# One kernel, attention and a gated feed-forward layer: the hand-written order of all engines reaches over three chunks of eight instead of two

## The chip, the cores and the metric

The kernel runs on one core of a Trainium2 chip. The metric is the device time of one execution in microseconds (us). A core has five engines with a queue each: TensorE (PE in the profile, its weight loads PEld), VectorE (DVE), ScalarE (ACT), GpSimd (POOL) and SyncE (SP, which here only issues DMAs). Each engine works through its own instructions in order; a semaphore makes one engine wait for another.

## What is computed

Local attention with block summaries, and behind it a feed-forward layer with a short convolution and a gate. 4 batches, 8 heads, 768 positions, 64 numbers a head; model width 512, inner width 1024.

```python
def _attn_ref(q, k, v):
    k_sum = k.reshape(B, H, nb, block, D).max(axis=3)       # block = 32
    v_sum = v.reshape(B, H, nb, block, D).mean(axis=3)
    scores_l = scale * np.matmul(q, k.transpose(0, 1, 3, 2))
    mask_l = np.abs(pos[:, None] - pos[None, :]) < window   # window = 16
    scores_s = scale * np.einsum('bhsd,bhnd->bhsn', q, k_sum)
    scores_s = scores_s + np.log(block)
    ...
    a = a / (np.sum(a, axis=-1, keepdims=True) + 1e-09)
    v_all = np.concatenate([v, v_sum], axis=2)
    return np.matmul(a, v_all)

def _moe_ref(x, w_in, conv_w, w_out):
    h = np.maximum(x @ w_in, 0.0)
    ...
    for k in range(K):                                       # K = 3
        conv_out += conv_w[k][None, None, :] * hp[:, k:k + S, :]
    gate = 1.0 / (1.0 + np.exp(-conv_out))
    return h * gate @ w_out
```

## The kernel before

**Tiling.** The work is cut into 8 chunks `c` of 384 positions, two for each batch. Attention of a chunk runs in four pairs of heads; pair `n` is numbered through all chunks, so pairs 0 to 3 belong to chunk 0, 4 to 7 to chunk 1, and so on (32 pairs). The feed-forward layer of a chunk runs in 8 units `u` of 128 inner columns. A product in float32 is made of three TensorE matmuls of rounded parts (high by high, high by low, low by high), so there are hi and lo copies of the weights, of the attention's result (`xh`, `xl`) and of the gated values.

**Steps.** The program is made of small steps, with a name and numbers each; one step is one call of a function:

- DMAs on SP's queue: `R` k, `T` v, `Q` q, `K` and `V` the windows of k and v, `M` the block means of v, `I` and `O` a piece of w_in or w_out, `C` the convolution's weights.
- weights, once: `z`, `lo`, `st` put a float64 word's two halves together (ScalarE, VectorE, VectorE), `hi` rounds (ScalarE), `wl` makes the low part (GpSimd). `wlo3` is w_out's fourth piece, `wli3` w_in's.
- attention of pair n: `ks` block maximum of k (VectorE), `win` and `kb` put window and block keys together, `vs` block sum of v (VectorE), `pv` its transposition (TensorE), `vm` the mean (ScalarE), `vb` (GpSimd). `qk` 24 score matmuls; six each of `mx` (mask and maximum, VectorE) and `ex` (exponential, ScalarE); `sm`, `rc`, `nr` normalise (ScalarE, VectorE, GpSimd or VectorE). `trJ` and `cpJ` with J = 2n, 2n+1 transpose a head and copy it out of PSUM (TensorE; ScalarE or VectorE); `av` 24 matmuls with v; `xh` and `xl` round the result (ScalarE, VectorE).
- feed-forward of chunk c, unit u: `f c.u.cc`, cc = 0 to 3, three matmuls each (L429); `re` the ReLU (ScalarE, L443); `ta` and two `cv` the three taps (ScalarE or VectorE L454, VectorE L463); `th` tanh (ScalarE, L474); `mu` the gate (VectorE, L481); `gh`, `gl` the two parts of the gated value (ScalarE L491, GpSimd L494).
- second product: `g st.u` three matmuls (L513) into output tile st of batch 0, `ob` its copy and store (ScalarE). A tile needs the units of the chunks that hold its 128 rows.
- `w n`: n matmuls on an idle tile into an unused PSUM tile.

A letter at the end of a name chooses the engine: a ScalarE, v VectorE, p GpSimd.

**Written order.** The string `ORDER` is a list of such steps. With `FIRST` = 2 the list holds the feed-forward steps of chunks 0 and 1, what they need, and attention as far ahead as a later unit expects it (qk up to pair 13, tr up to 24, av up to 11). `run` calls each step, and `tc.manual_schedule()` keeps the order of the list on every engine.

**Planner.** Chunks `FIRST` to 7 come from `unit`, eight units each. Unit u of chunk c has the number j = 8(c + 1) + 3 + u. `slot(j)` issues attention steps ahead: an even j the loads of pair j/2 + 2 and the scores of pair j/2, an odd j the loads and block sums of pair (j + 1)/2. `vs`, `pv`, `vm`, `ks` occur only for the first half of a batch (`at(n)[3] == 0`), that is pairs 16 to 19, 24 to 27 and so on. Then come four `f`, `re`, `ta`, `cv` and two to four steps of the second product. In these chunks only TensorE keeps the program's order; a planner, which works from its own costs, orders the other engines. In chunk `FIRST` the slot's steps carry an edge behind the last of the listed steps that return an instruction: the last DMA on SP, and the last `mu` on VectorE (`last`). In `unit`, for an odd j:

```python
            if c == FIRST:
                for x in last.values():
                    behind.enter_context(tc.issue_after(x))
            slot(j)
        ...
        elif c == FIRST and u == 0:
            slot_t(j)
```

So in chunk `FIRST`, unit 0, the order on TensorE is: what `slot(j)` puts there, then `slot_t(j)` (tr and cp of group j - 2), then the f steps.

**Buffers that matter.** PSUM: the f steps have three tiles (`f1`), scores two, the transposed weights (`pt`) one, `xp` and from pair 4 on `pv` one together (`x`), the second product one (`f2`). SBUF: tag `stage`, two buffers, holds w_out's pieces, v of odd batches' loads (`vt`) and one pair's keys in turn; `kw` three, `q` and `va` four, `kT` two, `t` three.

Of the kernel before, what the change touches and what calls it, by code (L numbers as in the profile page):

```python
# [58 lines left out]
ex4.1.2 mx5.0.0 cp6v nr3.1p vm3 av2 zo0 mx5.0.1 loo0 ex5.0.0 tr7 sto0 T8 xh2 f0.1.1 I5 cp7a
mx5.0.2 vb3 xl2 K7 hio0 mx5.1.0 wli4 ex5.0.2 w1 av3 Q7 mx5.1.1 vs9 ex5.0.1 ex5.1.0 f0.0.2  # L60
mx5.1.2 xh3 M4 loi7 f0.1.2 zi7 xl3 sm4 sti7 ex5.1.2 f0.0.3 O1 zi3 pv9 ed4 f0.1.3 loi3 re0.0 rc4
f0.2.0 sti3 R9 re0.1 ex5.1.1 nr4.0p ta0.0v f0.2.1 M5 ta0.1a cv0.0.0 kb6 hii3 tr8 nr4.1p f0.2.2
cv0.1.0 Q9 hii7 qk6 cv0.0.2 wli3 cp8a cv0.1.2 th0.0 f0.2.3 V4 sm5 mx6.0.0 th0.1 mu0.0 tr9 wli7
re0.2 mx6.0.1 f0.3.0 R8 mu0.1 zi5 mx6.0.2 M6 ta0.2a f0.3.1 loi5 Q8 mx6.1.0 cp9a rc5 f0.3.2 sti5
# [12 lines left out]
f1.2.0 zo4 mx9.1.0 f1.0.3 ex8.1.1 loo4 mx9.1.1 gh0.7 T10 f1.2.1 sto4 sm8 K11 re1.0 f1.1.3 rc8
gl0.7 vs11 ta1.0a f1.2.2 re1.1 g0.3 cv1.0.0 nr8.0p O5 hio4 mx9.1.2 M8 f1.2.3 gh0.6 cv1.0.2 kb10
V8 wlo4 ta1.1a pv11 ks11 tr16 ex9.0.2 qk10 th1.0 cv1.1.0 nr8.1p ex9.0.0 g0.4 mu1.0 ex9.1.1 gl0.6
cv1.1.2 cp16a f1.3.0 vm11 vs10 ex9.1.2 tr17 kb11 f1.3.1 th1.1 ex9.1.0 mx10.0.0 pv10 O7 mu1.1  # L80
f1.3.2 vm10 Q11 zo5 loo5 f1.4.0 V9 mx10.0.1 gh1.0 sto5 f1.3.3 M9 ex9.0.1 cp17v gl1.0 f1.4.1 K12
re1.2 mx10.0.2 V10 sm9 av8 ta1.2a rc9 mx10.1.0 Q12 nr9.0p ex10.0.2 mx10.1.1 cv1.2.0 Q14 f1.4.2
nr9.1p zo7 K13 cv1.2.2 tr18 f1.4.3 Q13 mx10.1.2 th1.2 loo7 qk11 hio5 mu1.2 xh8 cp18v wlo5 V11
f1.5.0 ex10.1.0 mx11.0.0 M10 tr19 xl8 ex10.0.1 f1.5.1 ex10.1.1 sto7 g0.5 hio6 K14 mx11.0.1 hio7
cp19v wlo6 f1.5.2 mx11.0.2 re1.3 av9 V12 mx11.1.0 ta1.3a mx11.1.1 wlo7 ex10.0.0 g0.6 cv1.3.0 V13
ex10.1.2 cv1.3.2 f1.5.3 M13 ex11.0.0 kb12 sm10 mx11.1.2 g0.7 gh1.2 rc10 M11 nr10.0p qk12 M12 ob0
gl1.2 th1.3 tr20 ex11.0.2 g1.0 mu1.3 K15 nr10.1p ex11.1.2 mx12.0.0 f1.6.0 cp20v ex11.1.1 kb13
gh1.3 g1.1 mx12.0.1 mx12.0.2 ex11.0.1 gl1.3 tr21 re1.4 f1.6.1 re1.5 ta1.4v g1.2 ex11.1.0 cv1.4.0
# [11 lines left out]
def attention_ffn(ctx, tc, qT, kT, vT, k_win, v_win, w_in, cwT, w_out, mask8, ident_in, out):  # L100
# [17 lines left out]
    idle = cp.tile([P, 512], mybir.dt.bfloat16, name="idle")  # L120
# [99 lines left out]
    def keys(n):  # L220
        if n not in kw:
            if n == NP - 1:
                t = sp.tile([P, 1024], F32, tag="stage", name=f"kw{n}", bufs=2)
# [49 lines left out]
        nc.vector.tensor_reduce(ks[b, p], kv, AX.X, ALU.max)  # L273

    def win(n):
        k = kt[n]
        k = bass.AP(tensor=k.tensor, offset=k.offset, ap=[list(k.ap[0]), [QB, CB], [1, WK]])
        (nc.gpsimd if n else nc.vector).tensor_copy(keys(n)[:, :, :WK], k)

    def kb(n):  # L280
        c, p, b, hf = at(n)
        nc.gpsimd.tensor_copy(
            keys(n)[:, :, WK:NK], ks[b, p].unsqueeze(1).to_broadcast([P, CB, NB])
        )

# [11 lines left out]
        nc.tensor.transpose(pvs[n][:NB, :P], vsum.pop(n), ident)

    def v_mean(n):
        c, p, b, hf = at(n)  # L300
        vm[b, p] = cp.tile([NB, P], F32, tag=f"vm{p}", name=f"vm{n}")
        nc.scalar.activation(vm[b, p], pvs.pop(n)[:NB, :P], AF.Copy, scale=1.0 / BLK)

    def vb(n):
        c, p, b, hf = at(n)
        nc.gpsimd.tensor_copy(
            va[n][WK:NK, :, :], vm[b, p].unsqueeze(1).to_broadcast([NB, CB, P])
        )

# [44 lines left out]
            accum_out=sm[n][:, h, i : i + 1],  # L354
        )

    def sums(n):
        nc.scalar.activation(sm[n], sm[n], AF.Copy, bias=1e-9)

    def rc(n):  # L360
        nc.vector.reciprocal(sm[n], sm[n])
# [50 lines left out]
    def xh(n):  # L412
        nc.scalar.copy(rows(n)[0], xp[n][:, :CH])

    def xl(n):
# [22 lines left out]
        hf = c % 2  # L438
        return CH - 1 + 2 * hf, (CH - 1) * hf

    def re(c, u):
# [1 line left out]
        nc.scalar.activation(h, h, AF.Relu)  # L443
# [46 lines left out]
    def gh(c, u):  # L490
        nc.scalar.copy(gate_rows("hi", c, u), conv[c, u])  # L491

    def gl(c, u):
        nc.gpsimd.tensor_tensor(  # L494
            gate_rows("lo", c, u),
            conv.pop((c, u)),
            gate_rows("hi", c, u).bitcast(F32),
            ALU.subtract,
        )
# [252 lines left out]
```

## Time and profile before

| what | value |
| --- | --- |
| time, median of 3 runs | 385.96 us (385.96, 385.96, 388.12) |
| the profiled execution | time 388.25 us, span 386.5 us, mean granted TensorE clock 0.987 |
| TensorE busy | 367.7 us (95%) in 3131 instructions |
| VectorE, ScalarE, GpSimd busy | 245.5 (64%), 250.4 (65%), 147.8 us (38%) |
| chain that ended last, largest shares | TensorE 74%, DMA 13%, VectorE 5%, ScalarE 5% |
| DMA | 56.35 MB, mean 146 GB/s over the span |

The span is the time from the first to the last instruction of the profiled execution; its time has 1.75 us around it. Busy shares are averages over very different stages, so the stretches of the span are read one by one. The page's second part shows this in 40 equal slices, each digit the busy share in tenths (PEclk is the granted TensorE clock, DMA the share of the 16 DMA engines):

```profile
PE   7787999989879999999989999999999999999996
DVE  4998999975875664786655555666656655465200
ACT  2996999978936877655577787666665743334211
PEclk9998999999969999999999999999999999999999
DMA  8999976898596445653332333242310000000011
```

Each digit stands for 9.7 us. Two slices have a lower clock, the fourth and the twelfth. In the first ten slices VectorE, ScalarE and DMA are about full; from the thirteenth on TensorE is.

### The profile page before, as it was taken

The page shows a single profiled execution, that of the slowest core. Times are in us where ns is not written, and L with a number is a line of the kernel's source. Part 1 is how long each engine was busy: PE and PEld are TensorE (multiplying, and loading weights), DVE is VectorE, ACT ScalarE, POOL GpSimd, SP SyncE. Part 2 cuts the span into 40 slices and gives each one's busy share as a digit, 9 for nine tenths or more (in the row PEclk, how much of TensorE's full clock was granted, in tenths as well). Part 3 has the DMA queues.
Part 4 walks back from the last instruction along what each step waited for, and adds up shares of the span by engine and source line. Part 5 has one row for each costly group of instructions (what it writes and reads, how often), then busy time and mean ns, then how long its engine had stood idle before and what let it go on. Part 6 is the DMA issues. An engine that isn't in the chain of part 4 may idle for free.

```text
span 386.5 us, 8769 instructions
## 1 busy us (share of the span) xinstructions
PE 367.7 (95%) x3131; PEld 314.4 (81%) x3135; DVE 245.5 (64%) x765; ACT 250.4 (65%) x796; POOL 147.8 (38%) x184
## 2 busy tenths in 40 slices
PE   7787999989879999999989999999999999999996
...
DVE  4998999975875664786655555666656655465200
ACT  2996999978936877655577787666665743334211
...
PEclk9998999999969999999999999999999999999999
DMA  8999976898596445653332333242310000000011
GB/s 290 380 323 366 278 256 217 263 309 241 155 307 189 130 140 152 189 162 111 98 122 92 119 97 125 68 124 76 105 65 2 30 24 5 27 30 27 27 56 54
DMA packets 27435, 56.35 MB, mean 146 GB/s; under 512 B 3136, under 2 KB 11520, under 8 KB 27392
## 3 DMA queue, kind: packets, MB, share of 16 engines
...
q14 instruction: 18, 0.15, 0.1%
...
## 4 chain that ended last, share of the span: by engine, by line
PE 74%; DMA 13%; DVE 5%; ACT 5%; issue 1%; POOL 0%; SPq 0%; ACTq 0%; DVEq 0%; POOLq 0%
PE f L513 31%; PE f L429 29%; DMA wo<-w_out 6%; PE xp L387 5%; PE pt L373 5%; PE pq L319 4%; DMA kw<-k_win 2%; DMA va<-v_win 2%; DVE t L463 2%; DMA raw_b<-vT 2%; ACT a L348 2%; ACT t L474 1%; DMA mask<-mask 1%; DVE t L481 1%; DVE ks L273 1%
## 5 line engine op out<-in xcount | busy, mean ns | idle before, releaser
L494 POOL TENSOR_TENSOR glo<-t,ghi 128x383 fp32r<-128x383 f32 (+1 forms) x64 | 65.0, 1016 | 121.2 <-ACT ghi L491 112.4
L429 PE MATMUL f<-xh,win_hi 128*128 128x384 f32 (+1 forms) x256 | 93.7, 366 | 0.6 <-DVE t L481 0.3
L429 PE MATMUL f<-xl,win_hi 128*128 128x384 f32 (+1 forms) x256 | 87.9, 343 | 0.0
L429 PE MATMUL f<-xh,win_lo 128*128 128x384 f32 (+1 forms) x256 | 87.6, 342 | 0.0
L463 DVE SCALAR_TENSOR_TENSOR t<-f,cw,t 128x382 f32<-128x382 f32 (+3 forms) x128 | 78.6, 616 | 13.5 <-ACT t L452 10.7
L348 ACT ACTIVATE a<-a,nm 128x120 f32<-128x120 f32 x192 | 73.7, 386 | 3.6 <-DVE nm L333 3.1
L513 PE MATMUL f<-wout_hi,ghi 128*128 128x512 f32 x192 | 75.9, 396 | 0.0
L513 PE MATMUL f<-wout_lo,ghi 128*128 128x512 f32 x192 | 75.4, 393 | 0.0
L513 PE MATMUL f<-wout_hi,glo 128*128 128x512 f32 x192 | 74.9, 391 | 0.0
L474 ACT ACTIVATE t<-t 128x383 f32<-128x383 f32 (+1 forms) x64 | 33.6, 525 | 44.8 <-DVE t L463 43.9
L365 POOL TENSOR_TENSOR a<-a,sm 128x360 f32<-128x360 f32 x61 | 48.5, 811 | 29.6 <-ACT f L443 16.5
L481 DVE SCALAR_TENSOR_TENSOR t<-t,f 128x383 f32<-128x383 f32 (+1 forms) x64 | 35.5, 554 | 31.0 <-ACT t L474 30.7
L429 PEld LDWEIGHTS f<-xh,win_hi 128*128 128x128 f32 x256 | 49.3, 192 | 5.6 <-DVE t L481 1.7
L429 PEld LDWEIGHTS f<-xl,win_hi 128*128 128x128 f32 x256 | 49.4, 193 | 1.3 <-DVE xl L417 0.2
L429 PEld LDWEIGHTS f<-xh,win_lo 128*128 128x128 f32 x256 | 49.2, 192 | 0.0
L333 DVE CUSTOM_DVE_ANT_0 a<-pq,mask 128x120 f32<-128x120 f32 x192 | 44.7, 276 | 0.7 <-PE pt L373 0.6
L513 PEld LDWEIGHTS f<-wout_hi,glo 128*128 128x128 f32 x192 | 36.2, 188 | 8.0
L443 ACT ACTIVATE f<-f 128x384 f32<-128x384 f32 (+1 forms) x64 | 30.3, 474 | 16.9 <-PE f L429 16.8
L513 PEld LDWEIGHTS f<-wout_hi,ghi 128*128 128x128 f32 x192 | 36.2, 189 | 5.9 <-ACT ob L523 0.3
L513 PEld LDWEIGHTS f<-wout_lo,ghi 128*128 128x128 f32 x192 | 36.3, 189 | 5.2
L373 PE MATMUL pt<-ident,a 128*120 128x128 f32 x192 | 33.2, 282 | 6.8 <-DVE aT L378 3.2
L491 ACT CAST ghi<-t 128x383 fp32r<-128x383 f32 (+1 forms) x64 | 32.6, 509 | 8.9 <-DVE t L481 8.6
...
## 6 DMA issues: line engine op xcount, KB each, us to landing
...
```

The costliest lines, as they stand in the source:

```text
L333: nc.vector.tensor_tensor_reduce(aa[n, h][:, i, :], pq[n][h][:, i * NK : (i + 1) * NK], mask[:, {(0, 0): 0, (1, 2): 2}.get((hf, i), 1), :] ...
L348: nc.scalar.activation(a, a, AF.Exp, bias=nm[n][:, h, i : i + 1], scale=-1.0, accum_out=sm[n][:, h, i : i + 1],)
L365: engine[e].tensor_tensor(a, a, sm[n][:, h, :].unsqueeze(2).to_broadcast([P, 3, NK]), ALU.mult)
L373: nc.tensor.transpose(pt[j][:NK, i * P : (i + 1) * P], a[:, i, :], ident)
L429: nc.tensor.matmul(f1ps[c, u][:, :n], w[:, u, cc, :], x[:, cc, :n], start=(cc == 0 and m == 0), stop=(cc == NCC - 1 and m == 2),)
L443: nc.scalar.activation(h, h, AF.Relu)
L463: nc.vector.scalar_tensor_tensor(t[:, i0:i1], f1ps[c, u][:, hf + k - 1 + i0 : hf + k - 1 + i1], cw[:, u, k : k + 1], t[:, i0:i1], ALU.mult ...
L474: nc.scalar.activation(t, t, AF.Tanh, scale=0.5)
L481: return nc.vector.scalar_tensor_tensor(t, t, 1.0, h, ALU.add, ALU.mult)
L491: nc.scalar.copy(gate_rows("hi", c, u), conv[c, u])
L494: nc.gpsimd.tensor_tensor(gate_rows("lo", c, u), conv.pop((c, u)), gate_rows("hi", c, u).bitcast(F32), ALU.subtract,)
L513: nc.tensor.matmul(f2ps[b, st], g[:, fc, ss], w[:, fc, :], start=(fc == 0 and m == 0), stop=(fc == NFC - 1 and m == 2),)
```

## The change

`FIRST` becomes 3 and the list is made anew, for chunks 0, 1 and 2. It has 1019 entries in place of 766 (counting the `w` entries, which stand for 38 and 35 idle matmuls). It is another order from its first steps on, not the old one with a tail. New in it are the steps of chunk 2, that is 32 f steps with all behind them, the second product's tiles 2 to 4 of batch 0 (`g2.*` to `g4.*`, `ob2` to `ob4`), the attention steps that the planner's slots 27 to 34 issued (qk 14 to 17, tr 25 to 32, av 12 to 15, the loads with them), and `ed12`. Chunks 3 to 7 come from `unit`, which is unchanged. The helper functions take an engine's letter in more places; the old engine is the default everywhere, and the new list has letters on `nr`, `cp` and `ta` alone, as the old list has. According to its description, chunk 3's first steps were weighed in the making of the new list.

```diff
-FIRST = 2
+FIRST = 3
...
-R0 Q0 R1 I0 I1 R2 Q1 ks0 R3 win0 Q2 kb0 qk0 T0 ks1 win1 C kb1 zi0 loi0 T1 mx0.0.0 ex0.0.0
...
+R0 R1 Q0 R2 I1 Q1 I0 win0 ks0 I2 Q2 ks1 T0 kb0 qk0 R3 kb1 ks2 win2 Q3 win1 mx0.0.0 ex0.0.0
...
+ta0.0v tr8 ex5.1.1 f0.2.3 cv0.0.0 ex5.1.2 ta0.1a loi7 cv0.0.2 kb6 hii3 nr4.1p w2 qk6 cv0.1.0 sm5
+th0.0 wli3 rc5 re0.2 cv0.1.2 zi7 mu0.0 cp8a sti7 w4 f0.3.0 ta0.2a wli4 mx6.0.0 th0.1 f0.3.1 vs11
+zo0 tr9 gh0.0 f0.3.2 mx6.0.1 O1 loo0 hii7 cv0.2.0 gl0.0 O2 f0.3.3 cp9a V4 mu0.1 ex6.0.1 nr5.0p
...
-f1.7.2 ta1.6a mx13.0.2 g1.5 ex12.1.2 cv1.6.0 xh10 tr23 cv1.6.2 gh1.5 g1.6 ex13.0.1 mx13.1.0
-gl1.5 xl10 f1.7.3 sm12 cp23a mx13.1.1 th1.6 g1.7 rc12 mx13.1.2 nr12.1p ex13.1.0 mu1.6 av11
-ex13.0.2 nr12.0p re1.7 gh1.6 ta1.7v tr24 ex13.1.2 gl1.6 cv1.7.0 ex13.1.1 ob1 cv1.7.2 th1.7 sm13
-xh11 rc13 mu1.7 nr13.1p xl11 gh1.7 nr13.0p cp24v gl1.7
...
+ob1 tr22 xl9 f1.7.2 mx13.0.0 gh1.4 cp22v g2.0 ta1.6a mx13.0.1 ex12.1.2 mx13.0.2 pv17 f1.7.3
+cv1.6.0 ex12.1.0 f2.0.0 vm17 sm12 gh1.5 rc12 av10 cv1.6.2 re1.7 gl1.5 vs16 tr23 M14 xh10 f2.0.1
...
+cv2.5.0 tr32 ex17.1.1 g4.6 cv2.5.2 ex17.0.0 ex17.1.2 cp32v f2.6.0 th2.4 g4.7 th2.5 mu2.4 xh15
+f2.6.1 mu2.5 xl15 f2.6.2 sm17 gh2.5 rc17 nr17.1p ob4 nr17.0p gh2.3 gh2.4 gl2.5 f2.6.3 re2.6
+gl2.4 ta2.6a gl2.3 cv2.6.0 cv2.6.2 f2.7.0 th2.6 f2.7.1 mu2.6 f2.7.2 f2.7.3 re2.7 gh2.6 ta2.7v
+gl2.6 cv2.7.0 cv2.7.2 th2.7 mu2.7 gh2.7 gl2.7
...
-    def hi(kind, fc):
-        nc.scalar.copy(parts(kind, fc)[0], wu[f"{kind}{fc}"].bitcast(F32))
+    def hi(kind, fc, e="a"):
+        copy[e](parts(kind, fc)[0], wu[f"{kind}{fc}"].bitcast(F32))
...
-    def re(c, u):
+    def re(c, u, e="a"):
         h = f1ps[c, u][:, : CH + 2 * (c % 2)]
-        nc.scalar.activation(h, h, AF.Relu)
+        if e == "a":
+            nc.scalar.activation(h, h, AF.Relu)
+        else:
+            nc.vector.tensor_scalar(h, h, 0.0, None, ALU.max)
```

The same form of edit is made in `wlo`, `win`, `kb`, `v_mean`, `vb`, `sums`, `xh`, `gh` and `gl`.

More of the change, by code (lines that the diff above doesn't have):

```diff
@@ L59 @@
[L59 to L64, printed above, removed]
@@ L77 @@
[L77 to L82, printed above, removed]
@@ L83 @@
[L83 to L88, printed above, removed]
@@ new lines @@
+mx9.0.0 ex8.1.1 ks10 gl0.4 pv8 f1.2.0 re1.0 sm8 g0.3 ta1.0a mx9.0.1 loo6 vm8 mx9.0.2 f1.2.1 zo6
+rc8 cv1.0.0 nr8.0p g0.4 re1.1 O7 mx9.1.0 cv1.0.2 ta1.1a kb10 M8 pv9 f1.2.2 nr8.1p mx9.1.1 gh0.7
+V8 cv1.1.0 tr16 th1.0 R11 gl0.7 f1.2.3 mx9.1.2 ex9.0.0 cv1.1.2 Q13 qk10 cp16a K11 mu1.0 th1.1
+sto6 f1.3.0 zo5 K13 mu1.1 tr17 re1.2 Q11 f1.3.1 hio6 loo5 M11 f1.4.0 sto5 zo7 T10 f1.3.2 vm9
+loo7 hio5 K12 f1.4.1 sto7 cp17a f1.3.3 ta1.2v wlo5 ex9.0.2 V11 ex9.1.0 av8 mx10.0.0 cv1.2.0
+ex9.0.1 V10 ex9.1.1 wlo6 ks11 g0.5 hio7 M9 f1.4.2 ex9.1.2 cv1.2.2 wlo7 g0.6 sm9 mx10.0.1 th1.2
@@ new lines @@
+Q12 mx10.0.2 gh1.1 f1.4.3 mu1.2 T17 ex10.0.1 rc9 g0.7 mx10.1.0 nr9.0p gh1.0 R17 mx10.1.1
+mx10.1.2 f1.5.0 kb11 ob0 gl1.1 vs10 V9 tr18 qk11 xh8 cp18v kb12 R16 ex10.0.2 g1.0 kb13 re1.3
+nr9.1p f1.5.1 ex10.1.1 K14 ta1.3a gl1.0 g1.1 gh1.2 cv1.3.0 f1.5.2 ex10.1.0 Q15 gl1.2 mx11.0.0
+cv1.3.2 g1.2 ex11.0.0 T16 ex10.1.2 mx11.0.1 tr19 mx11.0.2 th1.3 g1.3 mx11.1.0 re1.4 mu1.3
+ex10.0.0 f1.5.3 sm10 g1.4 ta1.4a rc10 mx11.1.1 nr10.0p cp19a mx11.1.2 f1.6.0 xl8 ex11.0.1
+cv1.4.0 qk12 re1.5 ex11.1.1 nr10.1v tr20 ta1.5a K15 pv10 f1.6.1 ex11.1.0 cv1.5.0 cp20a g1.5
@@ new lines @@
+xl10 ex13.0.1 kb15 gl1.4 tr24 g2.2 cp24v mx14.0.0 av11 mu1.6 mx14.0.1 tr25 cv1.7.0 xh11 V15 g2.3
+ex13.1.2 M12 xl11 f2.0.2 gh1.6 V13 cp25v ex13.1.0 g2.4 gl1.6 T18 mx14.0.2 ex13.0.0 mx14.1.0 K17
+cv1.7.2 f2.1.0 ex13.1.1 V14 mx14.1.1 sm13 f2.0.3 th1.7 Q17 rc13 nr13.0p ex14.0.1 pv16 mu1.7
+f2.1.1 ex14.0.0 mx14.1.2 g2.5 gh1.7 ex14.0.2 gl1.7 tr26 ex14.1.2 g2.6 re2.0 kb16 f2.2.0 ex14.1.0
+ta2.0v vm16 qk15 ex14.1.1 cv2.0.0 g2.7 mx15.0.0 nr13.1v f2.1.2 ob2 cv2.0.2 f2.2.1 ks17 f2.1.3
+cp26a th2.0 f2.2.2 mx15.0.1 kb17 mx15.0.2 re2.1 av12 sm14 ta2.1a tr27 V16 g3.0 mx15.1.0 M15
@@ new lines @@
+mx15.1.1 ex15.1.0 f2.2.3 mx15.1.2 Q18 cp27a mu2.0 g3.1 ex15.1.1 R18 rc14 nr14.0v re2.2 K18
+f2.3.0 xh12 nr14.1p ed12 M16 cv2.1.0 g3.2 ex15.0.1 R19 xl12 ex15.0.0 tr28 ex15.0.2 cv2.1.2
+f2.3.1 gh2.0 g3.3 ta2.2a gl2.0 th2.1 cv2.2.0 f2.3.2 ex15.1.2 qk16 g3.4 mx16.0.0 mx16.0.1 av13
+mx16.0.2 mu2.1 cp28v f2.3.3 M17 cv2.2.2 f2.4.0 K19 re2.3 g3.5 ex16.0.0 T19 sm15 V17 ex16.0.2
+tr29 th2.2 g3.6 mu2.2 f2.4.1 mx16.1.0 g3.7 mx16.1.1 rc15 mx16.1.2 nr15.1p cp29v f2.4.2 ob3
+nr15.0p f2.5.0 qk17 ex16.1.1 ta2.3a tr30 ex16.1.2 f2.5.1 mx17.0.0 gh2.1 mx17.0.1 g4.0 ex16.0.1
@@ new lines @@
+cv2.3.0 gl2.1 xh13 f2.5.2 gh2.2 xl13 f2.4.3 ex16.1.0 gl2.2 cp30v g4.1 sm16 re2.4 cv2.3.2 tr31
+rc16 mx17.0.2 g4.2 mx17.1.0 mx17.1.1 av14 ta2.4v nr16.1v g4.3 nr16.0v xh14 cp31a f2.5.3 xl14
+th2.3 cv2.4.0 g4.4 ex17.0.1 mx17.1.2 ex17.0.2 av15 cv2.4.2 re2.5 mu2.3 ta2.5a g4.5 ex17.1.0
+cv2.5.0 tr32 ex17.1.1 g4.6 cv2.5.2 ex17.0.0 ex17.1.2 cp32v f2.6.0 th2.4 g4.7 th2.5 mu2.4 xh15
+f2.6.1 mu2.5 xl15 f2.6.2 sm17 gh2.5 rc17 nr17.1p ob4 nr17.0p gh2.3 gh2.4 gl2.5 f2.6.3 re2.6
+gl2.4 ta2.6a gl2.3 cv2.6.0 cv2.6.2 f2.7.0 th2.6 f2.7.1 mu2.6 f2.7.2 f2.7.3 re2.7 gh2.6 ta2.7v
@@ L116, in attention_ffn @@
     raw_b = cp.tile([P, 6, 1024], U32, name="raw_b", tag="big_b")
+    engine = {"p": nc.gpsimd, "v": nc.vector}
+    copy = {"a": nc.scalar.copy, "p": nc.gpsimd.tensor_copy, "v": nc.vector.tensor_copy}
     idle = cp.tile([P, 512], mybir.dt.bfloat16, name="idle")
```

98 lines of the change are left out of this document (53 added, 45 removed).

## The prediction, as it was put on record

> **What bounds the kernel now.** I read the slices of the page first, then busy time in stretches cut at the kernel's own borders, then TensorE's instructions in order of time, then the chain that ended last. In the stretches PE, PEld, DVE, ACT and POOL are busy time, then come the granted TensorE clock, the DMA share and GB/s.
>
> ```profile
> core 0: us, PE busy (x) PEld busy (x) DVE busy (x) ACT busy (x) POOL busy (x), PEclk, DMA share, GB/s
> 25.96:40.05 14.09, 11.34 (x115) 9.79 (x116) 12.10 (x41) 10.56 (x40) 8.39 (x11) 0.88 1.03 343
> 40.05:80.95 40.90, 40.64 (x418) 34.78 (x416) 39.31 (x125) 38.88 (x122) 28.49 (x32) 1.00 0.82 257
> 80.95:103.20 22.25, 20.55 (x203) 16.81 (x203) 15.74 (x60) 19.87 (x69) 12.85 (x16) 1.00 0.78 231
> 103.20:108.64 5.44, 2.06 (x31) 1.28 (x29) 4.05 (x11) 4.16 (x15) 3.74 (x5) 0.86 0.80 203
> 108.64:113.37 4.73, 4.73 (x16) 4.73 (x17) 3.82 (x6) 0.48 (x1) 1.54 (x3) 0.50 0.92 322
> 113.37:154.72 41.35, 41.35 (x376) 36.15 (x375) 23.80 (x82) 30.44 (x98) 12.76 (x17) 0.99 0.52 162
> 154.72:199.80 45.08, 43.34 (x387) 38.47 (x386) 31.17 (x98) 27.85 (x93) 15.85 (x21) 1.00 0.47 140
> 199.80:243.35 43.55, 43.55 (x389) 38.40 (x388) 24.11 (x84) 32.20 (x102) 16.12 (x22) 1.00 0.32 102
> ```
>
> From 113 us on TensorE sets the pace: it is busy throughout, except in chunk 3. Ahead of that VectorE and ScalarE are as full (39.31 and 38.88 of 40.90 us). Time can be won only where TensorE stands still or runs at the lower clock. These places, in TensorE's order of time (start, duration, and in brackets the idle time before it and what ended it):
>
> ```profile
> 34.28 0.92 PE L387 MATMUL xp<-aT,va 120*64 120x64 f32 x24 [2.40 <-DVE xl L417]
> ...
> 61.20 0.42 PE L429 MATMUL f<-xh,win_hi 128*128 128x386 f32 x1
> ...
> 103.00 0.39 PE L513 MATMUL f<-wout_hi,ghi 128*128 128x512 f32 x1
> ...
> 104.90 0.54 PE L373 MATMUL pt<-ident,a 128*120 128x128 f32 x3 [0.19 <-POOL a L365]
> 108.64 0.89 PE L373 MATMUL pt<-ident,a 128*120 128x128 f32 x3 [3.19 <-DVE aT L378]
> ...
> 154.69 0.27 PE L297 MATMUL pv<-ident,vs 128*24 128x128 f32 x1
> 154.72 0.42 PE L429 MATMUL f<-xh,win_hi 128*128 128x386 f32 x1
> ...
> 194.62 0.52 PE L373 MATMUL pt<-ident,a 128*120 128x128 f32 x3 [1.75 <-ACT aT L378]
> ```
>
> At 61.20 chunk 1 begins (386 columns), at 103.00 its last f step, f1.7.3, is over, at 154.72 chunk 3 begins. The wait of 3.19 us is the hand-over from the written order to the planner: tr25 waits for cp24v, the last written VectorE step. After it the clock is at half. The chain that ended last gives the price (start, us, what), slow first and then the same two groups at full clock:
>
> ```profile
> 109.53 3.84 PE f L429 x12
> 113.37 2.38 PE f L513 x9
> ...
> 118.18 2.09 PE f L429 x12
> 120.27 2.08 PE f L513 x9
> ```
>
> 3.84 - 2.09 and 2.38 - 2.08, and 0.4 us for the slow tr25, make 2.4 us. With the idle 3.19 + 0.19 the old hand-over costs 5.8 us.
>
> **The change part by part.** *Helpers.* Every new letter has the old engine as its default, and the new list puts letters on nr, cp and ta alone, as the old one does: nothing.
>
> *The old hand-over goes.* After f1.7.3 the new list goes on with chunk 2's steps, so TensorE has work while VectorE and ScalarE finish chunk 1. I price the new stretch by its own content. Of TensorE it holds 32 f, 23 g, 4 qk, 6 av, 10 tr and one pv up to f2.7.3. Prices: f 2.09/4 = 0.52, g 2.08/3 = 0.69, and from the starts of these four rows tr 0.42, av 0.85, qk 0.78:
>
> ```profile
> 125.67 0.49 PE L373 MATMUL pt<-ident,a 128*120 128x128 f32 x3
> 126.09 0.92 PE L387 MATMUL xp<-aT,va 120*64 120x64 f32 x24
> 126.94 0.85 PE L319 MATMUL pq<-kw,q 64*64 64x120 f32 x24
> 127.72 0.54 PE L373 MATMUL pt<-ident,a 128*120 128x128 f32 x3
> ```
>
> That is 16.7 + 15.9 + 3.1 + 5.1 + 4.2 + 0.1 = 45.2 us. With pv18 and tr33, which come before f3.0.0, 45.7. The old stretch from 103.00 to 154.72 takes 51.7. So 6.0 us are to be had, if nothing new waits.
>
> *A new hand-over comes.* In `unit`, the first planned chunk traces its slot ahead of its f steps, and all of the slot's VectorE steps are queued behind the last written mu (`issue_after`). For chunk 2 that was slot 27, pair 14: q, v and a kb, nothing on TensorE. For chunk 3 it is slot 35, pair 18, the start of a batch's half: vs18 on VectorE and pv18 on TensorE. TensorE keeps its program order, so pv18 stands between f2.7.3 and everything else; in the row at 154.69 it stands in the same place, there with vs18 long done. Now pv18 waits for vs18, vs18 stands behind mu2.7, and mu2.7 hangs on f2.7.3 by re, ta, two cv and th. Behind pv18 are queued tr33, f3.0 and all of chunk 3. The same chain ran at the end of chunk 1 (first row re1.7; last the first vs after it):
>
> ```profile
> 103.70 0.48 ACT L443 ACTIVATE f<-f 128x386 f32<-128x386 f32 x1
> ...
> 104.29 0.62 DVE L454 TENSOR_SCALAR t<-f,cw 128x385 f32<-128x385 f32 x1 [0.51 <-ACT f L443]
> ...
> 104.94 1.27 DVE L463 SCALAR_TENSOR_TENSOR t<-f,cw,t 128x385 f32<-128x385 f32 x2
> ...
> 105.28 0.58 ACT L523 ACTIVATE ob<-f 128x512 f32<-128x512 f32 x1
> ...
> 106.37 0.53 ACT L474 ACTIVATE t<-t 128x385 f32<-128x385 f32 x1 [0.51 <-DVE t L463]
> ...
> 107.14 0.52 DVE L481 SCALAR_TENSOR_TENSOR t<-t,f 128x385 f32<-128x385 f32 x1
> 107.57 0.55 DVE L417 TENSOR_TENSOR xl<-xp,xh 128x384 fp32r<-128x384 f32 x1
> ```
>
> ```profile
> 108.93 0.94 DVE L288 TENSOR_REDUCE vs<-vt 128x24 f32<-128x768 f32 x1
> ```
>
> From the start of re to that of mu 107.14 - 103.70 = 3.44 us; the next VectorE step starts 0.43 later; vs takes 0.94; with 0.06 to hand over to TensorE 4.9 us. The list can add to it: on ScalarE th2.6 stands ahead of re2.7, and th2.6 is ready about 2.4 us after f2.6.3 (re and ta 1.1, two cv 1.27), while f2.7's four steps take 2.1; with th's own 0.4 re2.7 starts 0.7 us late. I take 5.5 us. Lower end 4.5 (nothing late); upper end 7.5, if ta2.6a waits for its buffer behind nr17.1p, nr17.0p and gl2.5 on GpSimd: this row's 1.53 for two nr, and one gl.
>
> ```profile
> 107.39 1.53 POOL L365 TENSOR_TENSOR a<-a,sm 128x360 f32<-128x360 f32 x2 [1.58 <-DVE sm L361]
> ```
>
> *The clock after it.* An idle 3.19 us was followed by half clock (0.50), 2.40 us too (mean 0.88 over 14.09 us, 1.7 us lost), 1.75 us not (1.00). So 5.5 us cost another 2.4; the lower end is 0. [...]
>
> *Chunk 2 as a written order.* The planner's chunks 4 and 5 run without a gap; a written order makes each engine wait in its fixed place. Chunk 1, written, has 37.9 us of TensorE work by these prices (32 f, 13 g, 5 qk, 5 av, 9 tr, 2 pv) and takes 103.00 - 61.20 = 41.8: 3.9 lost. It is crowded (39.31 and 38.88 of 40.90). The new stretch holds about what VectorE and ScalarE did from 103.20 to 154.72: 4.05 + 3.82 + 23.80 = 31.7 and 4.16 + 0.48 + 30.44 = 35.1 us for 45 of TensorE, 70 and 78%. I take 1.5, ends 0 and 4.7 (chunk 1's share of 3.9 in 37.9).
>
> *Chunks 0 and 1 in another order.* The work is the same, and up to f1.7.3 TensorE has g1.7 and g2.0 more and av10 and tr23 less, 0.1 us. What differs is where waits fall. The 2.40 us at 34.28 come from this step, which sat in VectorE's queue for w_out's first load:
>
> ```profile
> 31.23 1.48 DVE L155 TENSOR_SCALAR wl_o<-wo 128x512 uint32<-128x512 uint32 x1 [0.98 <-DMA wo<-w_out]
> ```
>
> The new list moves that step (loo0) behind chunk 0's third unit, which can save 2.4 and 1.7 of slow clock. Against it, six idle matmuls now stand ahead of f0.3.0 (1.3 us), where the list itself allows for a wait, the first loads go in another order on SP, and O5 and O7 keep some 5 to 7 us of TensorE work between issue and use, as before. I take -1.5; ends -5.8 (2.4 and 1.7 gone, and the 1.70 us that the stretch to 103.20 leaves idle) and +3 (a stall like the first, elsewhere).
>
> *Chunk 3 and later.* The moved loads (R, T, K, Q, V, M of pairs 14 to 19) land in a stretch where DMA is 0.52 busy: nothing, or a wait as long as one load if the cover fails. The 1.75 us at 194.62 come from a planner's choice, a ks that blocks VectorE behind a kb:
>
> ```profile
> 188.96 0.95 DVE L273 TENSOR_REDUCE ks<-kT 128x24 f32<-128x768 f32 x1 [1.09 <-POOL kw L282]
> ```
>
> It may come again or not: I take 0, ends -1.75 and +1.75.
>
> *Sum.* 45.7 + 5.5 + 2.4 + 1.5 = 55.1 against 51.7: +3.4; the head -1.5; later 0: +1.9 us. The profiled execution took 388.25 (span 386.5 and 1.75 around it), 2.3 above the median 385.96. The difference goes on the median: **387.9 us**. About 1% (3.9 us) is what a measurement of this kernel tells from no change, so this is "within 1%".
>
> **The rivals.** *Slower:* the written chunk 2 loses as chunk 1 does, 4.7 and not 1.5: 391.1. For it: one fixed order for five engines; against it: a third of ScalarE is free there. It decides from a loss of 3.5 us on. *Faster, no new stall:* vs18 is free of mu2.7, because the maker weighed chunk 3's first steps. Then 5.5 and 2.4 fall away: 380.0. Against it: the diff leaves `unit` as it is, and no TensorE step in the list stands behind f2.7.3 to cover the chain. *The head pays more:* -5.8 in place of -1.5: 383.6. For it speaks loo0's place, against it the stretch 40.05 to 80.95, where TensorE idles 0.26 us.
>
> **How the numbers follow.** Forecast 0.53 (its own range 385 to 390.5), slower rival 0.22, no stall 0.10, better head 0.15. Faster than 382.1: no stall, and a quarter of the better head: 0.14. Slower than 389.8: most of the slower rival and a quarter of the forecast's upper part: 0.30. Within: 0.56. The range 381.5 to 392 leaves out most of the no-stall case and the far ends.
>
> **What would show it.** Right: TensorE has no gap of 3 us near 103 to 109; its longest gap is 4.5 to 7.5 us, ends at a pv at L297 released by vs at L288, between the last 384-column f and the first 386-column one; half clock for some 4 us after it. Wrong: pv18 without a wait there, chunk 2 with more than 4 us of small gaps, or f1.7.3 over before 99 or after 106 us.

## The result and the profile after

Over 20 runs each, taken in turn, the changed kernel took 390.38 us at the median (387.01 to 392.64) and the kernel before 386.25 us (385.12 to 388.46). The ratio is 1.0098, 95% interval [1.0073, 1.0123]: about 1% slower, on the border between "within 1%" and "slower". The forecast was 387.9 in a range of 381.5 to 392. The two profiled executions took 392.09 and 388.25 us, so they differ by 3.84 us, much as the medians do (4.13), and can be compared stage by stage.

In the changed kernel the lines stand lower: f is L457, g L544, pv L318, vs L309, ks L294, kb L303, tr L401, re L472, ta L483 or L485, cv L494, th L505, mu L512, nr L393, gl L525. First its busy time in stretches cut at its own borders (columns as in the prediction):

```profile
core 0: us, PE busy (x) PEld busy (x) DVE busy (x) ACT busy (x) POOL busy (x), PEclk, DMA share, GB/s
...
101.90:148.10 46.20, 46.20 (x437) 38.92 (x436) 30.90 (x107) 31.31 (x110) 15.86 (x21) 1.00 0.57 176
148.10:155.50 7.40, 0.75 (x5) 0.65 (x5) 5.72 (x9) 2.96 (x7) 3.60 (x4) 0.66 0.00 1
155.50:161.50 6.00, 6.00 (x20) 5.61 (x19) 3.90 (x6) 1.02 (x3) 0.61 (x2) 0.56 0.87 268
```

The written chunk 2 (from 101.90 on) keeps TensorE busy without a break, where the old kernel had its hand-over. Then come 7.4 us in which TensorE works for 0.75, and 6 us at 0.56 of the clock. TensorE's instructions in order of time, with the idle time before them:

```profile
43.84 0.44 PE L457 MATMUL f<-xh,win_hi 128*128 128x384 f32 x1 [1.78 <-DVE t L512]
...
147.90 0.33 PE L457 MATMUL f<-xh,win_lo 128*128 128x384 f32 x1
...
154.88 0.37 PE L318 MATMUL pv<-ident,vs 128*24 128x128 f32 x1 [6.65 <-DVE vs L309]
...
155.55 0.67 PE L457 MATMUL f<-xh,win_hi 128*128 128x386 f32 x1
...
175.05 0.51 PE L401 MATMUL pt<-ident,a 128*120 128x128 f32 x3 [0.52 <-ACT aT L406]
...
198.43 0.52 PE L401 MATMUL pt<-ident,a 128*120 128x128 f32 x3 [1.72 <-ACT aT L406]
```

The longest gap, 6.65 us, ends at a pv that vs releases, between the last 384-column f and the first 386-column one. The chain that ended last runs through it (start, us, what); it shows on what vs itself waited:

```profile
144.93 0.19 DVE sm L389
145.29 1.54 POOL a L393 x2
146.82 0.98 POOL glo L525
147.82 0.59 ACT t L483
...
150.29 0.40 DVE t L512
150.76 0.62 DVE t L485
...
153.32 0.55 DVE t L512
153.88 0.87 DVE vs L309
...
154.88 0.37 PE pv L318
155.25 0.64 PE pt L401 x3
155.89 3.86 PE f L457 x12
159.75 2.61 PE f L544 x9
...
164.79 2.12 PE f L457 x12
166.91 2.06 PE f L544 x9
```

Read from the top: the normalisation of pair 17 on VectorE and GpSimd, a gl, then unit 6 of chunk 2 (ta at 147.82 to mu at 150.29), then unit 7 (ta at 150.76 to mu at 153.32), then vs18 and pv18. Two units' tails lie between the last f of chunk 2 and pv18, not one. The slow groups cost (3.86 - 2.12) + (2.61 - 2.06) = 2.3 us. The prediction's 2.4 counts a slow tr with them; here tr33 took 0.64 us in this chain (0.33 at full clock), and that 0.3 lies in the stretch ahead of the groups.

Chunk 4 starts at 203.67, 3.85 us later than before (199.82), and from there on both kernels run at the same pace. So the account of the 3.84 us, beside the prediction's terms:

| term | predicted | in the profile | worked out from |
| --- | --- | --- | --- |
| head, up to the end of chunk 1's f | -1.5 | -1.1 | f2.0.0 starts at 101.91; f1.7.3 was over at 103.00 |
| loss in the written chunk 2 | 1.5 | 1.0 | 46.2 us for 45.2 us of content |
| wait of pv18 | 5.5 | 6.65 | row at 154.88 |
| slow clock after it | 2.4 | 2.3 | chain |
| rest of chunk 3 | 0 | +0.7 | 48.12 - 45.10 - 2.3; of it 0.5 from the stalls (0.52 and 1.72, before 1.75), the rest small waits |
| stretch from chunk 1's last f to chunk 3 | 45.7 + 5.5 + 1.5 = 52.7 | 53.64 (51.72 before) | 155.55 - 101.91 |
| sum | +1.9 | +3.8 | -1.1 + 1.9 + 2.3 + 0.7 |

### The profile page after: what moved, and what is told of

It is laid out like the page before. It is cut to its first block, busy times and chain, and to the rows that moved or that the text cites. A ratio compares the mean times of both kernels' runs of the same rounds, so it can differ in the third digit from the quotient of the medians.

```text
span 390.3 us, 8750 instructions
## 1 busy us (share of the span) xinstructions
PE 371.5 (95%) x3138; PEld 315.2 (81%) x3138; DVE 252.1 (65%) x776; ACT 247.9 (64%) x790; POOL 144.5 (37%) x179
## 4 chain that ended last, share of the span: by engine, by line
PE 75%; DVE 11%; ACT 5%; DMA 3%; POOL 3%; issue 2%; SPq 1%; ACTq 0%; POOLq 0%; DVEq 0%
PE f L544 31%; PE f L457 29%; PE xp L415 5%; PE pt L401 5%; PE pq L344 4%; DVE t L494 3%; ACT a L373 2%; DVE t L512 2%; DMA kw<-k_win 1%; DMA k_xl<-kT 1%; POOL a L393 1%; DVE a L358 1%; ACT t L505 1%; DVE ks L294 1%; DVE xl L445 1%
## 5 line engine op out<-in xcount | busy, mean ns | idle before, releaser
L525 POOL TENSOR_TENSOR glo<-t,ghi 128x383 fp32r<-128x383 f32 (+1 forms) x64 | 64.7, 1014 | 129.4 <-ACT ghi L522 121.9
L457 PE MATMUL f<-xh,win_hi 128*128 128x384 f32 (+1 forms) x256 | 92.7, 362 | 2.0 <-DVE t L512 2.0
L457 PE MATMUL f<-xl,win_hi 128*128 128x384 f32 (+1 forms) x256 | 87.8, 343 | 0.1
L457 PE MATMUL f<-xh,win_lo 128*128 128x384 f32 (+1 forms) x256 | 87.7, 343 | 0.0
L494 DVE SCALAR_TENSOR_TENSOR t<-f,cw,t 128x382 f32<-128x382 f32 (+3 forms) x128 | 78.6, 614 | 13.4 <-ACT t L483 11.0
L544 PE MATMUL f<-wout_hi,ghi 128*128 128x512 f32 x192 | 77.1, 401 | 0.0
L544 PE MATMUL f<-wout_lo,ghi 128*128 128x512 f32 x192 | 75.5, 393 | 0.0
L544 PE MATMUL f<-wout_hi,glo 128*128 128x512 f32 x192 | 75.1, 392 | 0.0
L505 ACT ACTIVATE t<-t 128x383 f32<-128x383 f32 (+1 forms) x64 | 33.5, 524 | 45.0 <-DVE t L494 44.7
L393 POOL TENSOR_TENSOR a<-a,sm 128x360 f32<-128x360 f32 x56 | 44.4, 809 | 42.1 <-DVE sm L389 20.8
L457 PEld LDWEIGHTS f<-xh,win_hi 128*128 128x128 f32 x256 | 49.2, 192 | 7.4 <-DVE t L512 3.3
L512 DVE SCALAR_TENSOR_TENSOR t<-t,f 128x383 f32<-128x383 f32 (+1 forms) x64 | 35.3, 552 | 27.6 <-ACT t L505 27.3
L457 PEld LDWEIGHTS f<-xl,win_hi 128*128 128x128 f32 x256 | 49.3, 192 | 2.3 <-DVE xl L445 0.4
L457 PEld LDWEIGHTS f<-xh,win_lo 128*128 128x128 f32 x256 | 49.1, 192 | 0.0
L544 PEld LDWEIGHTS f<-wout_hi,glo 128*128 128x128 f32 x192 | 36.2, 188 | 8.0
L472 ACT ACTIVATE f<-f 128x384 f32<-128x384 f32 (+1 forms) x64 | 30.3, 474 | 18.6 <-PE f L457 18.5
L544 PEld LDWEIGHTS f<-wout_hi,ghi 128*128 128x128 f32 x192 | 36.4, 189 | 5.8 <-issue 0.5
L544 PEld LDWEIGHTS f<-wout_lo,ghi 128*128 128x128 f32 x192 | 36.3, 189 | 4.6
L485 DVE TENSOR_SCALAR t<-f,cw 128x385 f32<-128x385 f32 (+1 forms) x38 | 23.4, 617 | 25.5 <-ACT f L472 23.8
```

The lines of the kernel that those rows point to most:

```text
L393: engine[e].tensor_tensor(a, a, sm[n][:, h, :].unsqueeze(2).to_broadcast([P, 3, NK]), ALU.mult)
L457: nc.tensor.matmul(f1ps[c, u][:, :n], w[:, u, cc, :], x[:, cc, :n], start=(cc == 0 and m == 0), stop=(cc == NCC - 1 and m == 2),)
L485: nc.vector.tensor_scalar(t, h, cw[:, u, 1:2], 1.0, ALU.mult, ALU.mult)
L494: nc.vector.scalar_tensor_tensor(t[:, i0:i1], f1ps[c, u][:, hf + k - 1 + i0 : hf + k - 1 + i1], cw[:, u, k : k + 1], t[:, i0:i1], ALU.mult ...
L505: nc.scalar.activation(t, t, AF.Tanh, scale=0.5)
L512: return nc.vector.scalar_tensor_tensor(t, t, 1.0, h, ALU.add, ALU.mult)
```

## The experiments

The theory to test: the new hand-over (the wait of pv18 and the slow clock behind it) is what the change gives back. Rivals: the written chunk 2 or chunks 0 and 1 in the new order cost it; chunk 3 would be late anyway. The runs came in sets, each with its own runs of the kernel before (medians 386.93, 387.67 and 387.41 us), so kernels are compared by their ratio to it. The changed kernel's is 1.0098; it was not run again in these sets.

**vs18, pv18 and vm18 in the list.** They are issued among chunk 2's steps; the planner's slot leaves them out.

```diff
-... nr16.1v g4.3 nr16.0v xh14 ...
+... nr16.1v g4.3 nr16.0v vs18 xh14 ...
...
-... f2.7.0 th2.6 f2.7.1 ...
+... f2.7.0 pv18 th2.6 vm18 f2.7.1 ...
...
-                if at(n)[3] == 0:
+                if at(n)[3] == 0 and n != 18:
```

> Only pair 18's vs, pv and vm move: out of the planner's first slot into the list (vs18 ahead of xl14 on VectorE, pv18 between f2.7.0 and f2.7.1, vm18 behind th2.6). Theory: the 6.65 us idle ahead of pv18 in the changed kernel is pv18's wait for vs18, which is queued behind mu2.7. Then tr33 and f3.0 follow f2.7.3 at once, and with the gap goes the half clock (2.3 us). Next in line is qk18, whose key blocks (ks18, kb18) still stand behind mu2.7: mu2.7 ends 5.8 us after f2.7.3, ks18 and kb18 take 1.3 more, and TensorE has tr33, f3.0, three g steps, tr34 and av16 for that time, 5.9 us, so 1 to 1.5 us of waiting are left. 390.4 - 6.65 - 2.3 + 1.3 = about 382.7, ahead of the kernel before by 3.5. Rival: the tail of the list is late as a whole (two nr of pair 17 and three gl on GpSimd ahead of ta2.6a), so chunk 3's first steps wait for buffers and engines whatever pv18 does: a gap of 4 us or more stays in front of f3.0 or f3.1, time 387 or more.

Measured: 388.12 us, ratio 1.0037 [1.0005, 1.0069], neither kernel's time and far from the 382.7 expected. It is the rival's number, but not its mechanism: pv18 no longer waits (it stands at 146.16, f3.0.0 at 148.08, right behind chunk 2), but a bit later qk18 does, the scores of the same pair. The rows of its trace, VectorE's, GpSimd's and TensorE's together:

```profile
154.73 0.54 DVE L512 SCALAR_TENSOR_TENSOR t<-t,f 128x383 f32<-128x383 f32 x1
155.19 0.95 DVE L294 TENSOR_REDUCE ks<-kT 128x24 f32<-128x768 f32 x1
...
156.83 0.30 POOL L303 COPY kw<-ks 128x144 f32<-128x144 f32 x1
...
157.19 1.48 PE L344 MATMUL pq<-kw,q 64*64 64x120 f32 x24 [3.49 <-POOL kw L303]
...
193.36 0.51 PE L401 MATMUL pt<-ident,a 128*120 128x128 f32 x3 [1.92 <-ACT aT L406]
```

ks18 is the next VectorE step of the same slot, queued behind the same mu2.7; the kb and the qk of pair 18 hang on it. The wait had two layers, and taking away the first uncovered 3.49 us of the second, where 1 to 1.5 were expected: mu2.7 now ends 7.3 us after f2.7.3 and not 5.8, with ta and cv of chunk 3's first unit among its chain on VectorE, and kb18 stands behind a gl on GpSimd. Its price again includes the clock, at 0.50 for the next 3 us. Behind the stall of 1.92 us at 193 it fell too, as the stretch of busy time there shows (clock third from the end):

```profile
193.30:198.00 4.70, 4.64 (x18) 4.48 (x19) 2.75 (x18) 3.94 (x17) 1.37 (x2) 0.64 0.40 124
```

**The slot's key steps in the list too.** As above, and `ks18` behind `mu2.4`, `kb18` ahead of `cv2.6.0`; the slot skips them.

> As e1_vs18_listed, and ks18 and kb18 are in the list too (ks18 behind mu2.4, kb18 behind gl2.3), so nothing that TensorE needs for unit 0 and 1 of chunk 3 is queued behind mu2.7. Theory: the rest of 1 to 1.5 us ahead of qk18 goes as well: 381.0 to 382. Rival: no better than e1_vs18_listed, or slower by up to 1.5 us, since ks18 (0.9 us) now stands ahead of xl15 and the gate of unit 5 on VectorE and kb18 ahead of two gl on GpSimd, in the tail that is late already.

Measured: 380.45 us, ratio 0.9837 [0.979, 0.9884], a little below the expected 381.0 to 382. No idle time of TensorE over 0.6 us is left between chunk 1 and chunk 5, its mean granted clock is 1.0, and the stall near 195 us is gone as well. In stretches:

```profile
102.00:149.00 47.00, 47.00 (x444) 39.81 (x444) 33.15 (x110) 31.50 (x111) 15.78 (x21) 1.00 0.62 190
149.00:192.00 43.00, 42.98 (x385) 38.06 (x384) 33.39 (x101) 29.02 (x96) 16.55 (x23) 1.00 0.52 159
```

Chunk 4 starts at 191.96, 11.7 us ahead of the changed kernel. The first gap is 6.65, its clock 2.3, the two stalls of chunk 3 2.24: 11.2 of it. Why the stalls went as well is not shown. Chunk 2 is written in both kernels, the same but for the five steps put in, so its written order isn't what costs.

**VectorE's order edge alone.** `mu` doesn't return its instruction, so nothing makes the planner's VectorE steps wait for mu2.7; list and slot stay.

```diff
-        return nc.vector.scalar_tensor_tensor(t, t, 1.0, h, ALU.add, ALU.mult)
+        nc.vector.scalar_tensor_tensor(t, t, 1.0, h, ALU.add, ALU.mult)
```

> The list is as in the changed kernel; only the edge of the first planned chunk's VectorE steps behind the last mu falls away (mu returns nothing, so only SP's edge is left). Then the planner may put vs18, ks18 and what follows anywhere among the listed VectorE steps. Theory: the edge makes the wait; the gap of 6.65 us goes and the time falls by up to 9 us, less what the planner's own steps delay in the listed ones (each vs or ks is 0.9 us ahead of steps that TensorE waits for; a vs or ks put ahead of its load's landing can block the engine): 382 to 386. Rival (late tail): no change, 390.

Measured: 380.18 us, ratio 0.984 [0.9795, 0.9885], lower than the expected 382 to 386. The planner puts vs18, the first vs behind the listed vs17 and vs16, 33 us ahead of pv18, among chunk 2's steps:

```profile
115.55 0.94 DVE L309 TENSOR_REDUCE vs<-vt 128x24 f32<-128x768 f32 x1
...
148.98 0.27 PE L318 MATMUL pv<-ident,vs 128*24 128x128 f32 x1
```

pv18's row shows no wait. So one edge, on one engine, was the whole of the new hand-over.

**The same edit in the kernel before.** If the edge as such cost 6 us, the old kernel would gain too.

> The kernel before, list of two chunks, with the VectorE edge of the first planned chunk taken away as in e4_no_vector_edge. It asks whether the list's third chunk is worth anything in itself. Theory: the old hand-over waits for a listed step (cp24v behind a saturated ScalarE), which the edge does not touch, and no block sum stands in its first slot; so the time stays within 1 us of 386, and the 6 us by which e4_no_vector_edge beats it are the third listed chunk's. Rival: the edge is what costs time in both, and the old kernel gains as much: 380 to 382.

Measured: 387.07 us, ratio 0.9986 [0.9954, 1.0018]: no difference. Its hand-over stays, since there tr25 waits for a copy of chunk 1's last written steps and not for a planned one:

```profile
107.78 0.89 PE L373 MATMUL pt<-ident,a 128*120 128x128 f32 x3 [3.63 <-DVE aT L378]
```

The third listed chunk and the free VectorE together win the 1.6%; neither does alone.

**The clock measured by itself.** 28 matmuls on an idle tile behind f2.7.3 fill the gap ahead of pv18 and change nothing that vs18 hangs on.

```diff
-... f2.7.2 f2.7.3 re2.7 ...
+... f2.7.2 f2.7.3 wt28 re2.7 ...
...
+    def wt(n):
+        t = ps.tile([P, 512], F32, tag="f2", name="pw2", bufs=1)
+        for _ in range(n):
+            nc.tensor.matmul(t, idle[:, :P], idle, start=True, stop=True)
```

> The wait stays, but 28 idle matmuls stand behind f2.7.3 and fill some 6.0 of the 6.65 us, in a PSUM tile of the second product's buffer. They compute nothing that is used. If the half clock behind the gap comes from TensorE's idleness, f3.0 and the three g steps behind it run at full clock, and the time falls by what they lost, 2.3 us: 388.1. If the clock has another cause, the slow steps stay and the time is 390.4 or up to 0.5 above.

Measured: 389.59 us, ratio 1.0061 [1.003, 1.0093]. The execution that was profiled took 920.18 us, so its trace tells nothing of the others; the same kernel ran once more.

> The same kernel as e3_idle_matmuls, since the execution that was profiled there took 918 us and cannot be read. If TensorE's idleness sets the clock: half clock nowhere between f2.7.3 and the second unit of chunk 3, the twelve f and nine g matmul groups of unit 0 at 2.1 and 2.1 us, and a time 1.5 to 2.3 us below the changed kernel, 388 to 389. If not: 3.9 and 2.6 us for these groups, and 390 to 391.

Measured: 387.62 us, ratio 1.0005 [0.9971, 1.0038]. From TensorE's instructions (27 of the 28 are in the trace, and the added helper moves all lines by 5):

```profile
146.50 6.22 PE L154 MATMUL pw<-idle 128*128 128x512 bf16 x27
153.31 0.27 PE L323 MATMUL pv<-ident,vs 128*24 128x128 f32 x1 [0.60 <-DVE vs L314]
```

and from the chain that ended last:

```profile
153.91 2.12 PE f L462 x12
156.03 2.06 PE f L549 x9
```

pv18 still comes 6.7 us after the last f, but the next two groups run at full clock: the 2.3 us are the clock's alone. The two sets put the gain at 0.4 and 0.9% of the time (1.4 and 3.6 us), around the 2.3. The same kernel's ratio thus differs by 0.6% between two sets, and a smaller difference across sets tells nothing.

**gl ahead of the two nr.** The prediction's upper end blamed ta2.6a's wait on nr17.1p and nr17.0p ahead of it on GpSimd; here both go behind gl2.5.

```diff
-... rc17 nr17.1p ob4 nr17.0p gh2.3 gh2.4 gl2.5 f2.6.3 re2.6
-gl2.4 ta2.6a ...
+... rc17 ob4 gh2.3 gh2.4 gl2.5 f2.6.3 re2.6
+nr17.1p nr17.0p gl2.4 ta2.6a ...
```

> One exchange in the changed kernel's list: the two nr of pair 17 stand behind gl2.5 on GpSimd instead of ahead of it, and behind re2.6 in the list. It measures one part of the 6.65 us. Theory: ta2.6a waits 0.51 us for its buffer, which gl2.5 gives back only after the two nr (1.54 us); with gl2.5 first ta2.6a follows re2.6 at once and the whole chain to pv18 moves ahead by 0.5 us: gap 6.1 us. Rival: the wait is for another gl or for ScalarE's own queue (ob4, gh2.3, gh2.4 ahead of re2.6): gap 6.6 us as before. The time itself changes too little to be told (390).

Measured: 390.69 us in one run, from which no difference can be told. The gap ahead of pv18 is 6.85, not the 6.1 expected. From GpSimd's and ScalarE's rows:

```profile
143.74 1.00 POOL L525 TENSOR_TENSOR glo<-t,ghi 128x383 fp32r<-128x383 f32 x1 [8.09 <-DVE sm L389]
144.70 1.54 POOL L393 TENSOR_TENSOR a<-a,sm 128x360 f32<-128x360 f32 x2
...
146.25 0.58 ACT L483 ACTIVATE t<-f,cw 128x383 f32<-128x383 f32 x1 [0.37 <-POOL a L393]
```

ta2.6a now waits for the nr where it waited for the gl. It is a GpSimd wait in both, but which step really frees it stays open. GpSimd itself had idled 8.09 us before, and in the changed kernel 7.51 us, so it wasn't overloaded; there its first nr (at 145.29) waited for rc17 on VectorE (tile `sm`).

**Two buffers for each ks tile.** The stalls of 0.52 and 1.72 us in chunk 3 were put down to a ks that must wait for the kb of the one before.

```diff
-        ks[b, p] = cp.tile([P, NB], F32, tag=f"ks{p}", name=f"ks{n}")
+        ks[b, p] = sp.tile([P, NB], F32, tag=f"ks{p}", name=f"ks{n}", bufs=2)
```

> The changed kernel with two buffers for each ks (24 numbers a partition) instead of one. Theory on the idle 1.72 us at 198.4 us (1.75 in the kernel before): a ks of the next batch stands in VectorE's queue and waits for a kb, which read the old block maxima behind a window's load, and it blocks the gate behind it. With a second buffer the ks does not wait for the kb, VectorE's idle 1.08 us and TensorE's 1.7 us go: 388.7. Rival: the stall is ScalarE's order (twelve exponentials ahead of a copy that TensorE waits for) and stays: 390.4. The gap ahead of pv18 stays either way.

Measured, in the changed kernel: 387.56 us, ratio 1.0003 [0.9969, 1.0038]. The gap stays and both stalls of chunk 3 go (the 0.52 is missing from the trace with the idle matmuls too, which has one ks buffer, so it isn't shown to be the buffer's):

```profile
152.37 0.37 PE L318 MATMUL pv<-ident,vs 128*24 128x128 f32 x1 [6.63 <-DVE vs L309]
```

From the start of chunk 3 to that of chunk 4 its trace has 44.71 us against 48.12, 3.4 less: 2.24 for the stalls, and 1.3 because the slow groups were shorter (3.13 and 2.06). In the kernel before the same edit did not pay:

> The kernel before with two buffers for each ks tile: TensorE's stall of 1.75 us in chunk 3, put down to a ks that holds VectorE behind a kb, should go. Theory: 1.5 to 2 us less than before, ratio 0.995 to 0.996. Rival (the stall has another releaser, or comes back later): within 0.5 us, ratio 0.999 to 1.001.

Measured: 387.52 us, ratio 1.0008 [0.9984, 1.0031]: a miss. The 1.75 us stall is gone from its trace and chunk 3 took 43.67 us instead of 45.10, yet the median is no lower. In its trace chunk 4 starts 1.75 us earlier (198.07 for 199.82), and that execution took 386.76 us, one of the shorter of runs from 385.28 to 388.91. Why the others gained nothing stays open, and so does how much of the gain in the changed kernel is the buffer's.

**Both remedies with two ks buffers.**

> The listed slot (vs18, pv18, vm18, ks18, kb18 in the list) with two buffers for each ks tile. In the profile of the listed slot with one buffer VectorE still waits 2.0 us in all for a kb (longest 1.1), but TensorE had no gap left behind the written steps. Theory (the time follows TensorE's gaps alone): no more than 1 us less than the listed slot with one buffer, ratio 0.981 to 0.986 to the kernel before. Rival (VectorE's lateness is paid for at the end): the 2.0 us come off, ratio about 0.978.

> The changed kernel without VectorE's order edge from mu to the planned steps, and with two buffers for each ks tile. Theory (time follows TensorE's gaps, and none over 0.2 us was left behind the written steps): ratio 0.981 to 0.987, as without the second buffer (0.984). Rival (VectorE's 2.6 us of waits for a kb are paid for): about 0.977.

Measured: 381.74 us, ratio 0.9837 [0.9793, 0.9882], and 381.2 us, ratio 0.9846 [0.9808, 0.9884]. The ratios without the second buffer were 0.9837 and 0.984: no further gain. Waits of VectorE for a kb that reach no gap of TensorE cost nothing here.

**w_out's first piece later, in the kernel before.** The test of the prediction's head term.

```diff
-ex4.1.2 mx5.0.0 cp6v nr3.1p vm3 av2 zo0 mx5.0.1 loo0 ex5.0.0 tr7 sto0 T8 xh2 ...
+ex4.1.2 mx5.0.0 cp6v nr3.1p vm3 av2 mx5.0.1 ex5.0.0 tr7 xh2 ...
...
-... K7 hio0 mx5.1.0 ...
+... K7 mx5.1.0 ...
...
-... zi7 xl3 sm4 sti7 ex5.1.2 ...
+... zi7 xl3 sm4 sti7 zo0 loo0 ex5.1.2 sto0 T8 hio0 ...
```

> The kernel before with one piece of w_out's making (zo0, loo0, sto0, T8, hio0) moved some 25 steps later in the list of chunks 0 and 1, away from the place where TensorE idles 2.40 us at 34.28. The prediction's step (w_out's work there is what is paid for at the head): the idle time falls below 1 us and the last f of chunk 1 ends 1.5 to 3 us earlier, ratio 0.992 to 0.996. Rival (the chain of chunk 2's attention is late anyway, or the piece costs the same where it goes): the last f of chunk 1 within 1 us of its old place, ratio 0.998 to 1.003.

Measured: 388.16 us, ratio 1.0023 [0.9994, 1.0053], so by the time it is a miss: no gain. Its trace says otherwise: the 2.40 us at 34.28 are gone, the longest later idle time of chunk 0 is

```profile
37.96 0.54 PE L373 MATMUL pt<-ident,a 128*120 128x128 f32 x3 [1.07 <-POOL a L365]
```

and the last f of chunk 1 is over 1.9 us earlier, at 101.1. The profiled execution took 386.15 us, among the shortest of runs from 385.65 to 390.87; over all runs the time is no lower. So the place of these five steps made the stall; that it sets the time isn't shown.

## Why the prediction was right, and where it was off

*Its mechanism was right.* The old hand-over is gone; pv18 waits for vs18 behind mu2.7, at the named place, and half clock follows (0.50 from 154.88 to 158.00). The run without VectorE's edge shows that this wait is what the change gives back: 0.984 against 1.0098 is 2.6%, 10 us. The prediction's own rival without a new stall had put that case at 380.0; it was 380.18, at a median of 386.93 of the kernel before. That the two agree so closely is luck in part: in that trace (f2.0.0 at 102.82, chunk 3 from 149.33 to 192.92) the head gave 0.2 us and not 1.5, the stretch behind it 5.2 and not 4.5, and chunk 3, put at 0, gave 1.5. The rival's condition, a free vs18, wasn't met, for the reason the prediction gave: `unit` is unchanged.

*The hand-over's 5.5 us were too few* (6.65). The chain itself was well priced: from the start of re2.7 (150.17) to pv18 (154.88) 4.7 us, for 4.9. (The lower end of 4.5, "nothing late", lies below the chain's own 4.9.) What failed is the 0.7 us by which re2.7 was to start late, reasoned from th2.6 alone:

```profile
146.01 0.93 ACT L522 CAST ghi<-t 128x383 fp32r<-128x383 f32 x2 [0.41 <-ACT ob L554]
146.84 0.47 ACT L472 ACTIVATE f<-f 128x384 f32<-128x384 f32 x1
...
147.82 0.58 ACT L483 ACTIVATE t<-f,cw 128x383 f32<-128x383 f32 x1 [0.51 <-POOL glo L525]
...
150.17 0.47 ACT L472 ACTIVATE f<-f 128x384 f32<-128x384 f32 x1
```

The last f was over at 147.90 + 0.33 = 148.23, so re2.7 started 1.9 us late. The 1.2 us beyond the 0.7 arose a unit earlier, in two places at once. f2.6.3 was over at 146.15, but re2.6 started 0.7 us later, at 146.84, since ob4 and two gh stand ahead of it on ScalarE. Then ta2.6a waited another 0.51 us for a gl, as the upper end of 7.5 had it for GpSimd. The gl alone would have held ta2.6a to the same time, so a faster GpSimd could win only 0.5 of it with ScalarE's order as it is. The reason given there (GpSimd busy with two nr) did not hold up in the run that moved them, where re2.6 was late by as much.

*The clock term* (2.4) was right: 2.3, or 2.6 with the slow tr33 that it counts, and the idle matmuls took it away. *Chunk 2 as a written order* (1.5) measured 1.0, so the slower rival (4.7) falls. *Chunk 3 and later* (0) was +0.7, in its bounds.

*The head* (-1.5) came out at -1.1, but not for the reason given. The stall from w_out's first piece left its place at 34.28 and another one of 1.78 us came at 43.84, on a gate step (mu) queued on a full VectorE (busy for all 2.80 us from 41.00 on), 0.52 us of loo0 itself (at 42.28) among the steps ahead of it. After it the clock was low too, as the stretches show:

```profile
43.80:46.00 2.20, 2.16 (x11) 1.98 (x11) 2.20 (x7) 1.26 (x3) 2.20 (x2) 0.71 1.03 359
46.00:48.00 2.00, 2.00 (x9) 2.00 (x8) 2.00 (x8) 2.00 (x7) 1.15 (x2) 0.50 0.93 265
```

That is 0.29 x 2.2 + 0.5 x 2.0 = 1.6 us lost on top of 1.78, against 2.40 + 1.7 before. The stall moved rather than went, and the slow clock behind it is one execution's (see the last section). Moreover, f2.0.0 starts anywhere between 99.1 and 103.0 us in the profiles of kernels that share the new list, so a head term of 1 us can't be told from one execution to the next, and that -1.1 lies near -1.5 is luck.

The time itself was 2.5 us above the forecast (390.4 for 387.9): 1.15 of it from the wait, 0.7 from chunk 3, 0.4 from the head, less 0.5 from chunk 2 and 0.1 from the clock, which makes 1.65 of the 1.9 us between the profiled sums; the other 0.3 is pv18 and tr33, which ran slow (0.8 for 0.5). Another 0.3 came in because the median of before was 386.25 over the longer series and not 385.96, and 0.3 because the medians lie 4.13 us apart and the profiled executions 3.84.
